# Keeping each group of column-half matmuls together in a kernel that schedules itself

## The chip, the cores and the metric

The kernel runs on one core of a Trainium2 chip. The metric is the device time of one execution in microseconds. Before the change it was 297.04 us (median of three runs, 296.97 to 297.3). A program on one core has no second die to compare with, so a run counts as slow when it is over 1.5% above the fastest of the same kernel. The granted clock is the share of its full speed that TensorE was given; 1.0 is full.

## The reference, cut to what matters

```python
# q, k, v: (4 batches, 4 heads, 1088 positions, 32); S1, S2: (8, 32)
def phi(x):                                   # 64 features of a position and head
    a = np.einsum('rd,bhsd->bhsr', S1, x)
    b = np.einsum('rd,bhsd->bhsr', S2, x)
    return np.einsum('bhsi,bhsj->bhsij', a, b).reshape(*x.shape[:-1], r * r)
q_p, k_p = (phi(q), phi(k))
kv = np.einsum('bhsf,bhsd->bhfd', k_p, v)     # "k'v"
num = np.einsum('bhsf,bhfd->bhsd', q_p, kv)   # "numerators"
den = ...                                     # denominators
x = (num / den), heads side by side           # (4, 1088, 128)

theta = x @ w_theta                           # then a mixing over the positions
zr, zi = x * np.cos(theta), x * np.sin(theta)
y = np.einsum('ts,bsd->btd', w_tok_r, zr) + np.einsum('ts,bsd->btd', w_tok_i, zi)
u = x + y
return u + np.maximum(u @ w_ch, 0.0)
```

The inputs arrive as float64 and are converted on the chip. The largest is w_tok, 1088 x 1088 twice. Its 34 pieces become the tile `wT`, in three steps of ScalarE and two of VectorE each.

## The kernel before

The kernel doesn't issue its instructions as it names them. It records them as operations, with a cost and a due time each, and a small model of the engines' time then builds the order: the engine's next operation is the one that is due first among those that could start within WAIT of the earliest.

```python
class Operation:
    def __init__(self, engine, call, args, kw, n, cost, late, due):
        self.engine, self.call, self.args, self.kw, self.n = engine, call, args, kw, n
        ...
# duration(), the model's cost of an fp32 matmul: a 64-column half has its own
            return (n / 1200 + 0.03 if ins[0].shape[1] == 64 else max(0.22, n / 600)), 0.3
...
# lay_out(): the choice, and the issue at its end
                    t, op = min(((t, o) for t, o in starts if t <= first + self.WAIT),
                                key=lambda x: (x[1].due, x[1].n))
...
        for op in out:
            r = [x.real() if isinstance(x, View) else x for x in op.args]
            op.call(*r, **{k: x.real() if isinstance(x, View) else x for k, x in op.kw.items()})
```

Two kinds of matmuls use half of TensorE's columns: k'v and numerators. In both, the two halves n = 0 and n = 1 can run side by side (in the trace of the kernel before, those of a whole pair start 6 to 8 ns apart, and a whole numerator pair takes 0.79 us to the next start, where a half alone takes 0.80). A k'v group is six such matmuls (three chunks of 128 positions, two halves), and there are 12 groups, four batches by three. A numerator pair is two, and there are 12 pairs.

```python
            for i in range(GC):                       # keys_values: GC = 3
                for n in range(2):
                    c = g * GC + i
                    T.matmul(kv[n * 2 * D:(n + 1) * 2 * D], vn[:, c, 2 * n:2 * n + 2]...,
                             kp[:, i * H + 2 * n:i * H + 2 * n + 2]...,
                             start=(c == 0), stop=(c == NC - 1), tile_position=(0, n * 2 * D), ...)
...
        for n in range(2):                            # numerator
            T.matmul(xp[n * 2 * D:(n + 1) * 2 * D], kvbd[b % 2][:, n], qpT[n],
                     start=True, stop=True, tile_position=(0, n * 2 * D), ...)
```

## Time and profile before

| | before |
|---|---|
| span of the profiled run | 295.5 us |
| TensorE busy | 257.6 us, 87% |
| VectorE busy | 224.8 us, 76% |
| ScalarE busy | 166.0 us, 56% |
| granted TensorE clock, mean | 0.912 |
| chain that ended last | 74% TensorE, 15% VectorE, 7% ScalarE |

The lines behind this table stand in the prediction. In the trace's rows, TensorE's records of fp32 matmuls come two to a matmul (a row `x12` of k'v is six matmuls), except for transpositions (`w<-ident,...`), which are one each. All operations carry one source line, since a helper records them, so one goes by the tiles' names: `w<-feat,big` is k'v, `w<-fT,kvbd` numerators, `w<-wT,st` and `w<-wT,z` the mixing, `w<-ident,feat` the transposition of features.

### The profile page before, as it was taken

How to read it: one execution, taken by the hardware profiler on the slowest of the kernel's cores; microseconds unless marked ns; L12 is line 12 of the kernel's file. 1: busy time of each engine (PE TensorE's matmuls, PEld its weight loads, DVE VectorE, ACT ScalarE, POOL GpSimd, SP SyncE). 2: the span in 40 equal slices, each digit the busy share in tenths (PEclk: the TensorE clock that was granted, in tenths of full speed). 3: DMA queues.
4: the chain of work that ended last, by engine and by line, in shares of the span. 5: the costliest groups of instructions: out<-in, count | busy, mean ns of one | idle time of the engine just before them, and what ended most of it. 6: DMA issues, size and time to landing. Idle time of an engine off the chain costs nothing.

```text
span 295.5 us, 3773 instructions
## 1 busy us (share of the span) xinstructions
PE 257.6 (87%) x1255; PEld 168.1 (57%) x1255; DVE 224.8 (76%) x638; ACT 166.0 (56%) x326; POOL 0.7 (0%) x6
## 2 busy tenths in 40 slices
PE   4539584945599999999999999999999999999993
PEld 3426553524477656656565545677656666665671
DVE  5999999999998999979999447999881994421011
ACT  3696579999528999789992223226734004620000
POOL 0000000000000000000000000000000000000000
PEclk9957867775559999999999999999999999999999
DMA  7999115967002166753300000110000001000010
GB/s 252 384 355 353 21 67 201 332 239 226 0 0 83 31 205 220 223 151 106 131 1 27 27 2 0 41 36 1 23 2 0 27 0 29 22 0 0 27 29 22
DMA packets 11603, 28.77 MB, mean 97 GB/s; under 512 B 1216, under 2 KB 5568, under 8 KB 11584
## 3 DMA queue, kind: packets, MB, share of 16 engines
q1 hardware_dynamic: 11584, 28.53, 28.7%
q8 instruction: 10, 0.16, 0.2%
q14 instruction: 9, 0.07, 0.1%
HBM read 26.30 MB, written 2.23 MB: 97 GB/s over the span
## 4 chain that ended last, share of the span: by engine, by line
PE 74%; DVE 15%; ACT 7%; DMA 1%; issue 1%; ACTq 0%
PE w L344 74%; ACT step L344 3%; DVE big L344 2%; DVE wT L344 2%; DVE lv L344 2%; DMA big<-k_l 1%; ACT big L344 1%; DVE cut_r L344 1%; DVE ksl L344 1%; DVE feat L344 1%; ACT lv L344 1%; ACT wT L344 1%; ACT tn L344 1%; DVE cut_z L344 1%; ACT fT L344 1%
## 5 line engine op out<-in xcount | busy, mean ns | idle before, releaser
L344 PE MATMUL w<-wT,st 128*128 128x384 f32 (+1 forms) x384 | 130.9, 473 | 0.0
L344 PEld LDWEIGHTS w<-wT,st 128*128 128x128 f32 x384 | 68.3, 190 | 36.9 <-issue 5.2
L344 ACT ACTIVATE step<-st 128x544 f16<-128x544 f32 (+2 forms) x70 | 54.4, 827 | 5.7 <-DVE wT L344 5.6
L344 ACT COPY ot<-w 128x384 f32<-128x384 f32 (+2 forms) x16 | 6.0, 394 | 62.6 <-PE w L344 50.4
L344 DVE TENSOR_TENSOR uT<-xT,w 128x384 f32<-128x384 f32 (+1 forms) x12 | 6.4, 530 | 28.0 <-PE w L344 27.9
L344 PE MATMUL w<-feat,big 128*64 128x128 f32 x144 | 18.3, 325 | 7.5 <-DVE feat L344 7.5
L344 DVE CUSTOM_DVE_ANT_0 wT<-wT,step 128x1088 uint16<-128x1088 uint16 x34 | 24.3, 719 | 0.7 <-ACT step L344 0.3
L344 ACT ACTIVATE wT<-st 128x544 f32<-128x544 f32 x34 | 23.6, 713 | 0.4 <-DMA st<-w_tok 0.4
L344 ACT COPY fT<-w 128x384 f32<-128x384 f32 x36 | 16.2, 490 | 9.9 <-PE w L344 9.9
L344 ACT COPY lv<-w 128x384 f32<-128x384 f32 x36 | 16.1, 500 | 8.3 <-PE w L344 8.0
L344 PEld LDWEIGHTS w<-feat,big 128*64 128x64 f32 x144 | 11.1, 156 | 15.1 <-DVE feat L344 8.2
L344 PE MATMUL w<-ident,big 128*128 128x128 f32 x72 | 13.8, 346 | 6.7 <-ACT big L344 4.2
L344 PE MATMUL w<-s_bd,fT 128*128 128x64 f32 x72 | 13.7, 353 | 6.1 <-DVE s_bd L344 6.1
L344 PE MATMUL w<-mv,qsl 128*128 128x384 f16 (+2 forms) x108 | 16.2, 290 | 1.6 <-ACT lv L344 1.3
L344 PEld LDWEIGHTS w<-s_bd,fT 128*128 128x128 f32 x72 | 12.7, 264 | 6.9 <-DVE s_bd L344 6.2
L344 PEld LDWEIGHTS w<-ident,big 128*128 128x128 f32 x72 | 11.5, 185 | 8.4 <-ACT big L344 4.6
L344 DVE TENSOR_SCALAR wT<-wT 128x544 int32<-128x544 int32 x34 | 14.5, 435 | 0.4 <-ACT wT L344 0.3
L344 PE MATMUL w<-ksl 128*128 128x384 f16 x72 | 14.6, 362 | 0.0
L344 PEld LDWEIGHTS <-qsl 128*128 128x128 f16 x108 | 9.9, 99 | 7.8 <-issue 4.5
L344 PE MATMUL w<-fT,kvbd 128*64 128x384 f32 x48 | 13.3, 542 | 0.2 <-ACT fT L344 0.2
L344 DVE SCALAR_TENSOR_TENSOR tt<-tn,w 128x384 f32<-128x384 f32 x12 | 6.6, 552 | 8.6 <-ACT tn L344 8.4
L344 PE MATMUL w<-ident,feat 128*128 128x128 f32 x72 | 12.9, 302 | 0.3 <-ACT big L344 0.3
(190 smaller groups left out, 402.1 us busy)
## 6 DMA issues: line engine op xcount, KB each, us to landing
st<-w_tok SPq DMA_DIRECT2D x34, 544.0 KB, 4.9
big<-k_l SPq DMA_DIRECT2D x4, 576.0 KB, 4.9
big<-q_l SPq DMA_DIRECT2D x4, 576.0 KB, 3.9
big<-v_l SPq DMA_DIRECT2D x4, 576.0 KB, 5.4
out<-ot SPq DMA_DIRECT2D x8, 192.0 KB, 2.1
out<-ot SPq DMA_DIRECT2D x4, 128.0 KB, 1.8
st<-w_sq SPq DMA_DIRECT2D x1, 256.0 KB, 4.9
out<-ot SPq DMA_DIRECT2D x4, 32.0 KB, 1.8
```

What stands on the lines that cost most here:

```text
L344: op.call(*r, **{k: x.real() if isinstance(x, View) else x for k, x in op.kw.items()})
```

## The change

The intent: a group's matmuls become one operation of the scheduler, so nothing can be put between the halves that run side by side. Its tuned constants were tuned again.

```diff
-START = 101.9, 134.2, 165.1, 246.3
+START = 100.5, 125.1, 182.6, 273.6
-SOONER = {"denominators0": 4.5, "denominators1": -11, ...
+SOONER = {"denominators0": 78.5, "denominators1": -44.5, ...     (all entries are new; cut)
-PACE = 2.9
+PACE = 2.4
-    WAIT = 0.08
+    WAIT = 0.02
 class Operation:
-        self.engine, self.call, self.args, self.kw, self.n = engine, call, args, kw, n
+        self.engine, self.n, self.parts = engine, n, [(call, args, kw)]
...
-            return (n / 1200 + 0.03 if ins[0].shape[1] == 64 else max(0.22, n / 600)), 0.3
+            return max(0.22, n / 600), 0.3                    (a half has no cost of its own any more)
...
+    @contextmanager
+    def together(self, cost):
+        self.joined = []
+        yield
+        op, self.joined = self.joined[0], None
+        op.cost = cost
...
     def note(self, engine, fn, call, a, kw):
+        if self.joined:
+            op = self.joined[0]
+            op.parts.append((fn, a, kw))
+        else: ...                                            (a new Operation, as before)
...
-            op.stream = min(cost, math.prod(out.shape[1:]) * passes / 2400)
+            op.stream += math.prod(out.shape[1:]) * passes / 2400 * min(1.0, out.shape[0] / 128)
...
         for op in out:
-            r = [x.real() if isinstance(x, View) else x for x in op.args]
-            op.call(*r, ...)
+            for call, args, kw in op.parts:
+                r = [x.real() if isinstance(x, View) else x for x in args]
+                call(*r, ...)
...
+            with order.together(0.81):                       # around the six k'v matmuls
...
+        with order.together(0.85):                           # around the two numerator matmuls
```

## The prediction

> **What bounds the kernel now.** I read the page first: the busy shares and the slices, which also show the granted clock.
>
> ```profile
> PE 257.6 (87%) x1255; PEld 168.1 (57%) x1255; DVE 224.8 (76%) x638; ACT 166.0 (56%) x326; POOL 0.7 (0%) x6
> PE   4539584945599999999999999999999999999993
> DVE  5999999999998999979999447999881994421011
> ACT  3696579999528999789992223226734004620000
> PEclk9957867775559999999999999999999999999999
> ```
>
> There are two regimes. For about eleven slices (7.4 us each) VectorE is full and TensorE is half idle[...]. From slice 12 on TensorE never rests. The chain of waits and a table of stretches put the border near 77 us:
>
> ```profile
> 76.61 0.59 ACT big L344
> 77.24 47.45 PE w L344 x235
> ...
> 142.53 72.52 PE w L344 x344
> 215.08 74.06 PE w L344 x300
> ```
>
> ```profile
> 62.70:90.00 27.30, 17.83 (x79) 14.49 (x79) 27.14 (x86) 17.77 (x38) 0.00 (x0) 0.50 0.25 86
> 90.00:142.00 52.00, 51.73 (x274) 33.19 (x272) 47.86 (x104) 47.80 (x91) 0.00 (x0) 1.00 0.49 154
> ```
>
> The columns after the stretch are PE, PEld, DVE, ACT, POOL and the clock. In 90 to 142 us TensorE (51.7 of 52 us), VectorE (47.9) and ScalarE (47.8) are all nearly full: VectorE and ScalarE convert the 34 pieces of w_tok into wT, and the mixing of batch 0 follows close behind. Its last rows start as the last piece is done:
>
> ```profile
> 149.54 0.44 DVE L344 TENSOR_SCALAR wT<-wT 128x544 int32<-128x544 int32 x1 [0.25 <-ACT wT L344]
> 150.72 0.72 DVE L344 CUSTOM_DVE_ANT_0 wT<-wT,step 128x1088 uint16<-128x1088 uint16 x1
> ```
>
> ```profile
> 151.02 0.81 PE L344 MATMUL w<-wT,z 128*128 128x384 f32 x2
> ```
>
> So the end is the time at which TensorE gets enough work, plus TensorE's remaining work.
>
> **What whole and broken groups cost.** From TensorE's timeline (each fp32 matmul is two records):
>
> ```profile
> 110.89 0.87 PE L344 MATMUL w<-fT,kvbd 128*64 128x384 f32 x4
> 111.68 2.74 PE L344 MATMUL w<-wT,st 128*128 128x384 f32 x8
> ...
> 128.16 0.86 PE L344 MATMUL w<-fT,kvbd 128*64 128x384 f32 x2
> 128.96 0.83 PE L344 MATMUL w<-ksl 128*128 128x256 f16 x5
> ```
>
> A numerator pair left whole takes 111.68 - 110.89 = 0.79 us; one half of a broken pair takes 0.80 us alone. In the records the halves of a whole pair start 7 ns apart. For k'v, start to next start at full clock is 0.81 us for six (at 51.59 us), 0.58 for three, 0.37 for two, 0.36 for one. A lone one also slows its neighbour:
>
> ```profile
> 162.83 0.91 PE L344 MATMUL w<-wT,st 128*128 128x384 f32 x2
> 163.67 0.43 PE L344 MATMUL w<-feat,big 128*64 128x128 f32 x2
> ```
>
> 0.84 us from start to start, where such a matmul takes 0.65 inside a run.
>
> [...] the trace grants 0.50 through 62.7 to 90 us, after TensorE had waited 4.0 us (at 68.6) and before it waits 4.2 us (at 77.2).
>
> **The change, part by part.** No instruction is added or removed: each engine keeps its counts. The new order shows all 12 k'v groups as six matmuls in a row and all 12 numerator pairs adjacent; before, only 3 groups and 10 pairs were. The scheduler's constants (SOONER, START, PACE, WAIT, the costs of these operations) change too, and with them nearly the whole order on every engine.
>
> (a) Joining, in the stretch where TensorE is full. Batch 2's k'v (91 to 100.5 us) is in eight pieces: 0.31+0.37+0.58+0.37+0.59+0.37+0.58+0.58 = 3.75 us against 3 x 0.81 = 2.43: 1.3 us. Batch 3's (162 to 181 us) is nine single ones, two twos and a five: 9 x 0.36 + 2 x 0.37 + 0.80 = 4.8 against 2.4: 2.4 us. Two broken pairs of batch 1: 4 x 0.79 = 3.2 against 1.6: 1.6 us. Sum 5.3 us; slowed neighbours add some 1.5 us. Batches 0 and 1 would save 1 us before 77 us, where TensorE waits anyway.
>
> (b) The order. I summed durations down each queue: for every kind its median start-to-start time in the trace, for TensorE at full clock. This is arithmetic that I check on the kernel before. VectorE's sum to the first query feature of batch 0 is 81.0 us, which ended at 83.9; to the last wT piece 145.4, which ended at 151.4. TensorE's sum is 229.5 us in all, and start minus sum is 54.3 us at 90.4 us, 55.4 at 126.5, 56.3 at 153, 61.1 at 289.7: nearly constant, so TensorE lost nearly all its idle time before 90 us.
>
> In the new order VectorE's sum to the first query feature is 81.4 us: the head doesn't shorten, and TensorE's dense part again begins near 84 us. By then TensorE's queue has 31.0 us of work behind it, against 33.1 before. VectorE's sum to the last wT piece falls from 145.4 to 131.0, because keys' features of batches 1 and 2, two of batch 2's preparations and batch 1's numerators come after it. With the 4 to 5 us of waits seen before that is 135.5 us. ScalarE gives the same: 41 us of its work lie between the second piece of batch 1's query slices (some 92.5 us; before 91.7) and the last conversion step, so 133.6 us without one wait, 136 with before's 2 to 3 us.
>
> TensorE's new queue puts the last rows of batch 0's mixing after a sum of only 72.1 us. It can be there by 84.3 + (72.1 - 31.0) + 3 us of low clock = 128.4 us, but the wT pieces they need come at about 134.5 us. So TensorE starves about 6 us between 98 and 135 us. Start minus sum is then 62.5 us, where before had 55.8 at the same time.
>
> After that, VectorE's and ScalarE's sums run just ahead of TensorE: batch 2's keys are sliced at 140.1 + 5 = 145 us, where TensorE arrives at 147. I add 1 to 2 us of waits there. The drift to the end was 5 us; without broken groups some 3.3.
>
> Sum: new total 223.5, its last matmul starts at sum 222.6; 222.6 + 62.5 + 3.3 + 1.5 = 289.9 us, against 289.7 before. The tail (295.5 - 289.7 = 5.8 us) has the same instructions. The span is then 295.7 us, and 297 us with the 1.5 us between span and time (297.04 - 295.5). The saving of 6 to 7 us is real, and the starving takes it back. My sums for the wT chain are good to some 2 us and lean on waits copied from before; a schedule that was tuned again was probably tuned to something better, so I put the middle at 295.5.
>
> **Rivals.** *The saving shows in full* (289 to 291 us): TensorE bounds the kernel after 77 us, so 6.5 us off its work is 6.5 us off the end. For it: the chain is TensorE from 142 to 289 us. Against: the new order asks for wT 15 us sooner than VectorE and ScalarE delivered it, with both already at 92% in that stretch. *The new order keeps low clock longer* (300 to 303 us): TensorE pauses at 68 to 84 us again and then has only small matmuls and transposes, which in 77 to 90 us ran at 0.50[...]. *Waiting for the group's last input* costs: a whole group waits for one VectorE product, and all six had the same one before; so nothing.
>
> **Range and chances.** Two us on the wT chain, two on the waits after 135 us and one on the head make about 3 us of spread: 290.5 to 300.5. Two per cent is 5.9 us: faster than 291.1 needs rival one nearly whole, 0.15; slower than 303 needs the clock to fall as well, 0.04.
>
> **What would show it.** Joined groups: 0.81 and 0.80 us each, TensorE's busy time at full clock down by 5 to 7 us. The last wT add near 136 us instead of 151.4. TensorE waits for wT between 98 and 136 us adding to about 6 us, some hidden inside matmul records; the first query feature near 84 us. The prediction is wrong if wT is done by 131 us, if TensorE has no waits there, or if the dense part begins before 80 us (then faster), or if the clock is below 1.0 after 100 us (then slower).

## The result

The changed kernel takes 293.70 us (median of four runs, 292.15 to 294.78), against 297.14 us of the kernel before in the same rounds (296.97 to 297.3). The ratio is 0.988, with a 95% interval of 0.9835 to 0.9926: under 2%, and inside the predicted range. Ratios here are the mean time of one kernel's fast runs over that of the other's of the same rounds, so they are not quite the ratio of the medians quoted.

The page of the changed kernel, busy times and slices as before:

```profile
PE 243.5 (84%) x1255; PEld 160.0 (55%) x1255; DVE 226.4 (78%) x638; ACT 164.5 (56%) x326; POOL 0.7 (0%) x6
PE   4787962631067999999999999999999999999993
DVE  5999999999999899999999875798972993611011
ACT  4797859597299899997876214008734004720000
PEclk9959998595568899999999999999999999999999
```

TensorE is busy for 14.1 us less with the same 1255 records. Part of that is the joining; that less was done at half clock (the mean clock is 0.928, before 0.912) would be the other part, which I didn't separate. In the row of slices TensorE does more early on and nothing in slice 11 (73 to 80 us), and it is full from slice 14 on, before from slice 12. ScalarE has eight or nine tenths in slices 12 to 18, where it had 2 in slice 12 and 7 and 8 in slices 17 and 18. TensorE's timeline (start, length, operation, the idle time before it and what ended it) where its dense part begins:

```profile
82.01 2.18 PE L361 MATMUL w<-ident,feat 128*128 128x128 f32 x9 [10.62 <-DVE feat L361]
...
87.19 0.94 PE L361 MATMUL w<-w,xT 128*128 128x128 f32 x6 [0.70 <-ACT xT L361]
...
90.72 0.46 PE L361 MATMUL w<-mv,qsl 128*128 128x192 f16 x3 [1.13 <-ACT qsl L361]
...
92.16 0.53 PE L361 MATMUL w<-mv,qsl 128*128 128x384 f16 x3 [0.64 <-ACT lv L361]
...
97.76 1.46 PE L361 MATMUL w<-wT,st 128*128 128x384 f32 x4
...
101.61 0.82 PE L361 MATMUL w<-feat,big 128*64 128x128 f32 x12
102.36 0.55 PE L361 MATMUL w<-ident,big 128*128 128x128 f32 x3
```

A whole k'v group is one row of twelve records with 0.75 us to the next start. The first transposition of a query feature starts at 82.01 us. In the kernel before it starts at 84.13 us, and no pause follows it up to 98 us:

```profile
84.13 1.91 PE L344 MATMUL w<-ident,feat 128*128 128x128 f32 x8
...
98.00 0.91 PE L344 MATMUL w<-mv,qsl 128*128 128x384 f16 x6
```

In the changed kernel come four waits for ScalarE (the fourth is of 0.35 us at 93.04). The clock is 0.50 in 65.5 to 86.0 and again in 92.8 to 96.2 us. From 97.76 us on TensorE has no pause until 132.52 us, and that one is of 0.24 us:

```profile
132.52 0.38 PE L361 MATMUL w<-dg,ones 8*128 8x8 f32 x2 [0.24 <-ACT fT L361]
```

The last wT addition of VectorE starts at 132.81 us (150.72 before):

```profile
132.81 0.72 DVE L361 CUSTOM_DVE_ANT_0 wT<-wT,step 128x1088 uint16<-128x1088 uint16 x1
```

The chain of waits, here its pieces around the border (start, length, what):

```profile
130.08 0.82 ACT step L361
...
132.15 0.33 ACT fT L361
...
132.52 68.10 PE w L361 x386
```

Before, TensorE carried most of the chain from 77 us on. Now ScalarE's conversions and copies carry most of it from 97 to 132.5 us (one load of w_tok stands in it with 6.0 us, before 130.08; ScalarE worked meanwhile and paused for 0.36 us), and TensorE only after that. A table of the stretch from 78 to 131 us (length, then busy time of PE, PEld, DVE, ACT, POOL, then clock, DMA share and GB/s), first before, then after:

```profile
78.00:131.00 53.00, 52.73 (x267) 35.61 (x266) 49.09 (x114) 43.07 (x85) 0.00 (x0) 0.89 0.37 118
```

```profile
78.00:131.00 53.00, 46.11 (x205) 29.43 (x206) 50.77 (x95) 51.52 (x90) 0.00 (x0) 0.89 0.58 198
```

ScalarE is busy 51.52 of 53 us. In this stretch the new order does more of w_tok's conversion and less of TensorE's work: VectorE ends 23 of the 34 pieces between 78 and 131 us, before 13, and between 78 and 98 us 8, before 4.

To see where time is won or lost, I use the prediction's measure: the start of a TensorE operation minus the sum of all full-clock TensorE work queued before it. It grows only when TensorE waits, is slow, or loses time to its neighbours. The work of each kind of matmul is its median time to the next start at full clock.

| at | before | after | difference |
|---|---|---|---|
| first transposition of a query feature (84.1; 82.0 us) | 51.1 | 51.1 | 0 |
| about 98 us | 54.5 | 58.7 | +4.2 |
| about 133 us | 55.7 | 59.2 | +3.5 |
| last matmul (289.7; 285.8 us) | 61.1 | 63.3 | +2.2 |

The sum itself fell from 228.6 to 222.6 us at the last matmul. So 6.0 us of work went and 2.2 us of other loss came: 3.8 us, and the spans differ by 295.5 - 291.6 = 3.9 us. The new order loses its 4 us between 82 and 98 us, and gets some 2 us of them back later.

### The profile page after: what moved, and what is told of

Same layout as the page of the kernel before. It is cut to its first block, busy times and chain, and to the rows that moved or that the text cites.

```text
span 291.6 us, 3787 instructions
## 1 busy us (share of the span) xinstructions
PE 243.5 (84%) x1255; PEld 160.0 (55%) x1255; DVE 226.4 (78%) x638; ACT 164.5 (56%) x326; POOL 0.7 (0%) x6
## 4 chain that ended last, share of the span: by engine, by line
PE 55%; DVE 24%; ACT 13%; DMA 4%; issue 3%; SPq 0%; ACTq 0%; DVEq 0%
PE w L361 55%; ACT step L361 6%; DVE big L361 3%; DVE wT L361 3%; ACT wT L361 2%; DMA st<-w_tok 2%; DVE feat L361 2%; DVE lv L361 2%; DMA big<-k_l 2%; ACT tn L361 2%; DVE cut_r L361 2%; DVE m L361 1%; DVE cut_z L361 1%; ACT qsl L361 1%; DVE ksl L361 1%
## 5 line engine op out<-in xcount | busy, mean ns | idle before, releaser
L361 PE MATMUL w<-wT,st 128*128 128x384 f32 (+1 forms) x384 | 127.5, 473 | 0.0
L361 PE MATMUL w<-mv,qsl 128*128 128x192 f16 (+2 forms) x108 | 18.7, 324 | 13.2 <-DVE mv L361 11.0
L361 PEld LDWEIGHTS <-qsl 128*128 128x128 f16 x108 | 11.3, 108 | 19.9 <-issue 14.5
L361 PEld LDWEIGHTS w<-ident,feat 128*128 128x128 f32 x72 | 8.9, 152 | 15.4 <-DVE feat L361 11.3
L361 DVE TENSOR_REDUCE m<-big 128x4 f32<-128x1152 f32 x8 | 10.7, 1347 | 2.3 <-DMA big<-k_l 2.3
L361 PE MATMUL w<-s_bd,fT 128*128 128x64 f32 x72 | 11.7, 300 | 0.8 <-ACT ks L361 0.6
L361 PE MATMUL w<-w,xT 128*128 128x128 f32 x72 | 11.3, 294 | 0.8 <-ACT xT L361 0.7
L361 PEld LDWEIGHTS w<-w,xT 128*128 128x128 f32 x72 | 10.0, 203 | 3.5 <-ACT xT L361 1.8
L361 PEld LDWEIGHTS w<-ident,big 128*128 128x128 f32 x72 | 9.3, 159 | 4.8 <-DMA big<-k_l 2.8
L361 PEld LDWEIGHTS w<-s_bd,fT 128*128 128x128 f32 x72 | 10.5, 214 | 2.4 <-ACT ks L361 1.1
```

## The experiments

Theory A says that joining pays directly where TensorE is full, and that the new order costs some of it. Rival B says that the new constants bring the gain and the lone halves were hidden. Theories D to H are about the loss between 82 and 98 us. Each call of runs timed the kernel before on the same chip (its median was 296.6 to 297.4 us), so I compare ratios. For the changed kernel the ratio is 0.988. The kernel before takes from 296.3 to 298.9 us, mostly near 296.6 or 298.5 us; so medians can move by half a microsecond, and one profiled run is not the median.

### 1. The old order, groups joined in place

```diff
+        last = {op.group: i for i, op in enumerate(out) if op.group}
+        joined = {}
+        for op in out:
+            joined.setdefault(op.group, []).append(op)
+        out = [x for i, op in enumerate(out) if not op.group or i == last[op.group]
+               for x in (joined[op.group] if op.group else [op])]
         for op in out:                       # the issue, as before
```

Each k'v group and each numerator pair carries a label. Its early members move back to its last one. Assertions in the code hold that no operation passed over depends on a moved one or reuses its buffers.

> The kernel before with its order on every engine kept, but each k'v six and each numerator pair put together where its last member stood. Theory A (joining pays directly where TensorE is full): from the first query feature on, TensorE's summed full-clock work falls from 196.6 to 191.2 us, and four fewer wide matmuls follow a lone half (some 0.19 us each), so 5.4 to 6.2 us off the time: 290.9 to 291.7 us, 2 us faster than the changed kernel, whose new order would then have cost that much. Rival B (the lone halves lay in time in which TensorE would have waited anyway; the gain of the change is from its new constants): 296 to 298 us. Rival C (an early member that moves back to its group's last one delays what waits for the group, or the released slots): slower than 298 us.

Measured: 292.17 us (290.87 to 292.8, six runs), ratio 0.982 (0.978 to 0.985; the limit of 2% lies inside, so the verdict is unclear between "faster" and "same"). Of the expected 5.4 to 6.2 us, 5.2 came. Batch 3's k'v, whose pieces before were nearly all single:

```profile
166.69 0.88 PE L355 MATMUL w<-feat,big 128*64 128x128 f32 x12
167.49 1.56 PE L355 MATMUL w<-wT,st 128*128 128x384 f32 x4
...
169.74 0.88 PE L355 MATMUL w<-feat,big 128*64 128x128 f32 x12
```

Theory A stands, with no constant changed; B and C fall. This kernel's median is also 1.5 us below the changed kernel's. Its interval and the changed kernel's (0.978 to 0.985, and 0.983 to 0.993) overlap a little, so I call it at least as good, and not shown to be faster.

### 2 and 3. Only k'v, only the numerators

The same edit, with the label on one kind only.

> The kernel before with only the k'v sixes put together in place. TensorE's work from the first query feature falls from 196.6 to 192.8 us (3.8 us), and four fewer wide matmuls follow a lone half (0.8 us). Theory A: 3.8 to 4.6 us off 297.4, so 292.8 to 293.6 us, most of what both parts gave (5.2 us). Rival: if only the numerator pairs' joining counts, 297 us.

Measured: 293.69 us, ratio 0.988 (0.985 to 0.991), against 297.0 us: 3.3 us off, a little under the 3.8 to 4.6 expected.

> The kernel before with only the two broken numerator pairs put together in place. TensorE's work falls by 2 x 0.80 = 1.6 us, no slowed neighbours change. Theory A: 295.8 us (1.6 us off 297.4), and the two parts together make up the 5.2 us of both. Rival: the pairs are broken where TensorE waits for wT anyway (one lone half stands at 128 us): 297 us.

Measured: 295.79 us, ratio 0.995 (0.992 to 0.998): 1.2 us off, expected 1.6. The parts add up to 4.5 us, both together gave 5.2. By the ratios, which use means, it is 3.7 and 1.6 us, together 5.3, against 5.4 for both: the parts add up. Each part pays by itself, and k'v pays most.

### 4. Joined, with the old constants

```diff
-START, SOONER, PACE, WAIT of the changed kernel
+START, SOONER, PACE, WAIT of the kernel before
```

> The changed kernel's code with the old SOONER, START, PACE and WAIT: groups are joined, but the scheduler builds an order that was never tuned. TensorE's work from the first query feature is 192.2 us (before 196.6, changed 192.6). Theory A: 291 to 295 us, the 4.4 us of work less or more some 2 us for an order that isn't tuned. Rival B (the new constants bring the gain): 296 us or more.

Measured: 316.88 us (315.3 to 318.26), ratio 1.065. Neither expectation holds: the groups are whole, TensorE's summed work is the same 223.5 us as in the changed kernel, and the time is 20 us longer than before. TensorE's timeline shows where the first of it goes:

```profile
82.63 0.90 PE L360 MATMUL w<-ident,big 128*128 128x128 f32 x3 [8.75 <-ACT big L360]
88.37 2.51 PE L360 MATMUL w<-ident,feat 128*128 128x128 f32 x9 [3.13 <-DVE cz L360]
```

The first query feature is transposed at 88.4 us, and start minus sum grows from 66.5 at 136 us to 80.0 at 192 us, where the kernel before grew by 3 (TensorE pauses for 7.3 us there and has two stretches of 3.4 us at half clock). I had taken "an order that isn't tuned" for a matter of 2 us. It is one of 20. So a scheduler that works with whole groups needs other constants than the old ones, though the new ones don't bring the gain.

### 5. Split, with the new constants

```diff
 kernel before
-START, SOONER, PACE, WAIT of the kernel before
+START, SOONER, PACE, WAIT of the changed kernel
```

> The kernel before (every half an operation of its own, with its old costs) with the new SOONER, START, PACE and WAIT. The scheduler then breaks seven of 12 k'v groups and five pairs. TensorE's work from the first query feature is 198.1 us against the changed kernel's 192.6, and 13 wide matmuls follow a half instead of 5. Theory A: 5.5 + 1.5 us more than the changed kernel, 299 to 302 us. Rival B (the gain is the constants'): 293 to 295.5 us.

Measured: 306.46 us (306.27 to 307.03), ratio 1.030. B falls again. A's direction holds and its size is short by 4 us or more. Start minus sum is 61.0 at 105 us and 69.5 at 280 us, against 58.7 and 62.5 in the changed kernel, so here too the order suffers beyond the broken groups. Constants tuned for one granularity don't carry to the other, either way.

### 6. The new order, groups broken at issue

```diff
-        for op in out:
-            for call, args, kw in op.parts:
+        (a joined operation's first part is issued at its place; part j is issued after the
+         j-th later TensorE operation, or at once when an operation comes that depends on it
+         or takes over one of its buffers)
```

> The changed kernel with its order kept, but each group broken where it is issued: between two halves comes the next other matmul of TensorE, wherever nothing depends on the half and no buffer that it reads is reused in between. 43 of 72 k'v halves then stand alone and all 24 numerator halves. TensorE's work from the first query feature rises from 192.6 to 207.5 us, and nine more wide matmuls follow a half (0.19 us each). Theory A: 15 to 17 us more than the changed kernel, 308 to 311 us. Rival B (halves are hidden): 293 to 297 us. If it is well under 308, TensorE's dense stretch holds idle time that the records hide.

Measured: two fast runs, 317.35 and 317.27 us (ratio 1.066), two slow ones, and the profile is of a slow one (323.1 us). More than A expected. The profile shows that A was right for what follows the first query feature and wrong before it. The timeline, first the new wait's end, then broken groups:

```profile
94.88 2.18 PE L379 MATMUL w<-ident,feat 128*128 128x128 f32 x9 [10.61 <-DVE feat L379]
...
115.94 0.43 PE L379 MATMUL w<-feat,big 128*64 128x128 f32 x2
116.30 0.91 PE L379 MATMUL w<-wT,st 128*128 128x384 f32 x2
117.15 0.43 PE L379 MATMUL w<-feat,big 128*64 128x128 f32 x2
```

A lone k'v matmul takes 0.36 us to the next start, and the wide one after it 0.85 us. From the first transposition to the end of the span it is 321.2 - 94.9 = 226.3 us, against 291.6 - 82.0 = 209.6 us: 16.7 us more, and the expectation's 14.9 + 9 x 0.19 was 16.6. The other 12.9 us come before: VectorE's waits from 20 to 70 us add to 12.3 us, 6.6 of them in two waits for one product of TensorE (in the changed kernel they add to 0.2 us). I had counted broken groups in the head as free, since TensorE has idle time there. That was wrong, because VectorE, which has next to none, waits for their result. As the trace is of a slow run and the fast ones are some 6 us shorter, neither share is exact. The clock is 1.0 from 98.9 us on, so the slow run's lower clock (mean 0.904, in the fast ones 0.934 and 0.935) lies before that; an estimate for the head of the fast runs is 317.3 - 293.7 - 16.7 = 6.9 us.

### 7 and 8. Filler matmuls against the low clock, in the changed order

```diff
                 op = T.transpose(tr[:, i * P:(i + 1) * P], ...)      # first query feature
+                if (b, g, n, i) == (0, 0, 0, 0):
+                    op.parts[:0] = [(nc.tensor.matmul, (tr[:, :P], ident, ident),
+                                     dict(start=True, stop=True))] * 22      # then: * 38
```

> The changed kernel with 22 matmuls of the identity by itself put before the first transposition of a query feature (their result is overwritten), in the 10.6 us in which TensorE waits there (71.4 to 82.0 us). Theory D (the changed kernel's own loss between 82 and 97 us is low clock, granted 0.50 through 82 to 86 and 92.8 to 96.2 us[...]): the clock is 1.0 from about 79 us on, and 1 to 3 us come off: 291 to 292.7 us. Rival E (VectorE and ScalarE, not the clock, set when TensorE gets its work there): the clock rises and the time stays at 293.7 us. If the filler's end comes after 82 us or its slot frees late: slower.

> The changed kernel with 38 instead of 22 identity matmuls. The 22 took 6.85 us and left 4.0 us of idle time before the first query feature, and the clock fell back to 0.50 for 81.8 to 85.2 us. Sixteen more at 0.22 us fill 3.5 us of that. Theory D: the clock stays at 1.0 through 82 to 96 us and another 1 us comes off the 293.2 us of the shorter filler, 292 us or less. Rival E: the clock stays up and the time is within 0.5 us of 293.2 us, because VectorE and ScalarE set the pace there. If the filler ends after 82 us: slower by what it is late.

Measured: 293.17 us, ratio 0.986 (0.983 to 0.989), and 293.15 us, ratio 0.987 (0.984 to 0.990). Neither is distinguishable from 0.988, though the intervals don't exclude a gain of a microsecond. The long one's timeline:

```profile
71.22 10.50 PE L361 MATMUL w<-ident 128*128 128x128 f32 x76
82.03 1.48 PE L361 MATMUL w<-ident,feat 128*128 128x128 f32 x9 [0.32 <-DVE feat L361]
84.13 1.22 PE L361 MATMUL w<-fT,kvbd 128*64 128x384 f32 x4 [0.62 <-ACT fT L361]
...
87.22 0.94 PE L361 MATMUL w<-w,xT 128*128 128x128 f32 x6 [1.39 <-ACT xT L361]
```

The clock was 1.0 through 75.1 to 92.2 us (without filler it is 0.50 in 65.5 to 86.0 us, and TensorE's records fill 4.68 of the 20.30 us from 65.6 on) and the nine transpositions took 1.48 instead of 2.18 us. Then TensorE waited for ScalarE that much longer: the xT product starts at 87.22 us, with low clock at 87.19. Rival E holds: the clock was not what kept TensorE back there. (The short filler had 1.0 also in 92.8 to 96.2 us, and its trace is 1.2 us ahead at the first wT matmuls, 96.52 against 97.76. Its six runs don't confirm a gain of that size.)

### 9 and 10. Filler matmuls in the joined old order

```diff
+            for _ in range({210: 9, 232: 12}.get(count, 0) if op.engine == "PE" else 0):
+                self.nc.tensor.matmul(r[0], ident, ident, start=True, stop=True)
             # second form: {210: 9, 232: 10}, into tile[:, 384:] of the tile written last
```

> The kernel before with both kinds of groups joined in place, and with filler matmuls of the identity in its waits: nine before the key transpositions for which TensorE waits 4.2 us until 76.6 us, twelve before the first transposition of a query feature. There the clock was 0.50 from 62.1 to 89.4 us. Theory D: the clock is 1.0 from about 76 us on, TensorE's work from 83.5 to 89.4 us (6 us at half speed) shrinks by up to 3 us: 289.2 to 291 us. Rival E (VectorE, full from 66 to 91 us, sets the pace there): 292.2 us as without the filler. If the clock doesn't rise and the filler stands in the way (2.6 to 5 us of matmuls before 83.5 us): 293 us or more.

> As the joined kernel with filler before, with the filler where it waits for no buffer: nine identity matmuls into the unused columns of the tile that TensorE wrote last, before the key transpositions for which it waits until 76.6 us, and ten before the first query feature. Theory D: the nine run from 72.3 to 76.3 us, the clock is 1.0 from about 76 us on, the ten fit before 83.5 us, and the 6 us of work at half speed after that shrink by 1.5 to 3 us: 289.2 to 290.7 us. Rival E (VectorE sets the pace up to 91 us): 291.7 to 292.5 us, as joined without filler. If the first filler runs on past 76.6 us, it holds up VectorE as in the last trial and costs 1 us or more.

Measured: 297.73 us, ratio 1.001, and 294.22 us, ratio 0.990, against 0.982 without filler. Both cost time, by my placing. In the first the filler started only at 77.72 us, after TensorE's wait of 4.22 us for ScalarE that it was meant to fill, and VectorE then waited 3.13 us for TensorE. In the second the first nine ran at once (72.75 us), and the clock went from 0.51 in 71.8 to 75.2 us to 1.00 after it. It was 0.50 again from 82.0 us on, after 3.40 us in which short matmuls filled 2.34 us, and the ten others ran at that clock from 83.98 to 88.36 us, in the way. Theory D was not tested there as I meant to. What both runs do show is that a delay of TensorE before its dense part is paid for at the end, in part: the first transposition of a query feature came 8.1 us later (91.67 against 83.52) and the time grew by 5.6 us; in the second it came 4.8 us later (88.36), and the time grew by 2.1 us.

### 11. The first query features sooner, in the changed order

```diff
+        dve = [op for op in out if op.engine == "DVE"]
+        for n in (278, 280, 282, 284, 286, 288, 289):      # dn, dn, rd, rd, fl, feat, feat
+            op = dve[n]
+            out.remove(op)
+            out.insert(out.index(dve[277]), op)            # before six wT operations
```

> The changed kernel with seven operations of VectorE issued earlier: the steps from the denominators to the first two query features of batch 0 come before the six wT operations among them (start to next start 0.35 + 0.63 + 0.63 + 0.29 + 0.35 + 0.63 = 2.9 us), which then end 2.9 us later at the most. Theory F (VectorE's queue up to the first query feature sets when TensorE's dense part starts, and nothing after it takes that back): the first feature starts near 78.1 instead of 81.0 us and the time falls by 2 to 3 us, 290.7 to 291.7 us. Theory G (the prediction's wT chain has no slack: TensorE reaches the last rows of batch 0's mixing at 130 us, when wT is done at 133 us, so what comes sooner at 82 us is waited for there): within 1 us of 293.7 us, with new waits for wT, or for ScalarE behind it, between 100 and 135 us.

Measured: 295.58 us (295.17 to 296.78), ratio 0.996. Both expectations miss. VectorE had the features 2.1 us sooner, and TensorE lost 2 us:

```profile
79.87 2.18 PE L369 MATMUL w<-ident,feat 128*128 128x128 f32 x9 [8.46 <-DVE feat L369]
87.34 1.91 PE L369 MATMUL w<-fT,kvbd 128*64 128x384 f32 x4 [5.28 <-ACT fT L369]
```

The copies fT stand in ScalarE's queue behind conversions of w_tok, and these waited for the wT operations that I had moved back. ScalarE's timeline has both:

```profile
81.71 2.78 ACT L369 ACTIVATE step<-st 128x544 f16<-128x544 f32 x4 [11.02 <-DVE wT L369]
...
86.84 0.82 ACT L369 COPY fT<-w 128x384 f32<-128x384 f32 x2
```

TensorE had written what the first of these copies reads by 82.1 us. So ScalarE ran this copy 4.7 us after it was ready, when the conversions before it in the queue were done.

### 12. Half of the conversion, in the changed order

```diff
+        light = (from 77 us on: ScalarE's two step conversions, VectorE's shift and addition of w_tok)
+        half = lambda x, op: x.real()[:, :x.shape[1] // 2] if op in light else x.real()
```

Its output is wrong, which doesn't matter for the time.

> The changed kernel with its order kept and a wrong result on purpose: from 77 us on, ScalarE's two step conversions and VectorE's shift and add of each piece of w_tok treat half of the columns only. TensorE's work is the same. Theory H (VectorE and ScalarE, full from 78 to 133 us with 51 and 52 of 53 us busy, set when TensorE's dense part starts, so the wT work pulled forward into 77 to 97 us is where the new order loses its 4 us): the first query feature comes 1 us sooner, ScalarE's copies for TensorE two to three us sooner, the first two wT matmuls of the mixing (97.8 us) start 2 to 4 us sooner, and since TensorE is full from there on, the time falls by as much: 290 to 291.5 us. Rival E2 (the loss there is TensorE's own low clock, or a chain that doesn't run over wT): 293 to 294 us. If TensorE starts sooner but then waits again for something before 135 us, the gain is smaller than the shift at 97.8 us.

Measured: 290.01 us (289.49 to 290.68), ratio 0.977 (0.974 to 0.979).

```profile
81.13 2.18 PE L365 MATMUL w<-ident,feat 128*128 128x128 f32 x9 [9.34 <-DVE feat L365]
...
94.33 1.46 PE L365 MATMUL w<-wT,st 128*128 128x384 f32 x4
```

The first wT matmuls start 97.76 - 94.33 = 3.4 us sooner, and the time is 3.7 us shorter. The table of the stretch from 78 to 131 us has ScalarE at 42.14 and VectorE at 44.73 us. Theory H stands. TensorE's work and its order were the same, so half of the conversion held TensorE back by 3.4 us at 82 to 98 us. Part of that can come through the clock, which had no second stretch of 0.50 here: where the short filler alone took that stretch away, the first wT matmuls started 1.2 us sooner. And the same cut was not tried in the old order, so how much conversion costs there is not shown; that order ends 4 pieces between 78 and 98 us, the new one 8. (This is no version to keep.)

## Why the prediction was right

The time: 293.7 us against 295.5. By its own steps:

**Joining pays in work.** Right. The sum fell by 6.0 us, and every group is whole: 0.75 to 0.81 us for six k'v, 0.80 for a pair at 139.55 us. Experiments 1 to 3 put 5.2 us of time to it in the old order, 3.3 for k'v and 1.2 for numerators taken singly. The neighbours' 1.5 us was too much. A wide matmul of 384 columns took 0.10 us longer for each side on which a half stood (0.65 us inside a run, 0.75 and 0.84 in the kernel before), beside a whole group as beside a lone one (0.74 us at 169.00 us in experiment 1); the 0.84 us that the prediction read had halves on both sides. Summed over the wide matmuls at full clock, what they take beyond runs of their like fell from 3.4 to 2.8 us, and to 2.6 us in experiment 1.

**The head doesn't shorten.** Right only in what it brings. The first transposition came at 82.0 us, 84.1 before, "near 84" predicted: VectorE had the feature 2 us sooner, though its sum had grown by 0.4 us. Its waits up to there were 3.3 us, before 4.5, and the rest is not explained. But TensorE had 2.1 us less work behind it then, so start minus sum is 51.1 us in both kernels and nothing was won.

**wT sooner.** Nearly: the last addition starts at 132.8 and ends at 133.5 us, where the prediction put 135.5. Its sum of 131.0 us was good. What failed is the 4 to 5 us of waits taken over from before; they were 2.5.

**"So TensorE starves about 6 us between 98 and 135 us."** This step failed as it was put. TensorE is busy throughout that stretch, and start minus sum grows by 0.5 us. The prediction itself named "no waits there" as a sign against it. The loss is 4.2 us and lies before: between 82 and 98 us, in 2.8 us of waits for ScalarE and half-speed work. The reason behind the step was right, the new order asks more of VectorE and ScalarE sooner. The mistake was to add up wT as a queue of its own, with TensorE running ahead to its end. ScalarE serves both in one queue: the copies without which TensorE can't go on stand between conversions (in experiment 11 a ready copy waited 4.7 us for them). So TensorE was held at the beginning and reached late pieces of wT just as they came: it has no pause there but the 0.24 us for a copy of ScalarE, and in experiment 7's trace a matmul of the mixing starts at 129.77 us, 0.05 us after the wT addition that released it. In four runs of this order (experiment 11's has the seven operations moved) its first wT matmuls started at 96.5, 97.5, 97.8 and 99.8 us, and the last wT addition 34.9 to 35.1 us later each time. Experiment 11 shows the queue, and 12 that the conversion is what holds TensorE, with the limits said there.

**The drift to the end.** 3.3 + 1.5 us predicted from there, 63.3 - 59.2 = 4.1 us measured.

**The sum.** The arithmetic gave 297 us, and "a schedule that was tuned again was probably tuned to something better" put the middle at 295.5. The error of 297 - 293.7 = 3.3 us is start minus sum at 133 us, 62.5 predicted and 59.2 measured. It is the term of wT and starving that was too large, by the waits and by the start of TensorE's part. Two smaller errors cancel: the drift was 0.7 us less than predicted, and the profiled run's time is 2.1 us above its span, not 1.5. That the middle came nearer than the sum is luck: the guess about tuning rests on no step.

**The clock.** The prediction sets the stretch of 0.50 beside TensorE's waits that ended at 68.6 and 77.2 us. The clock had fallen before both, at 62.8 us, after a stretch (59.3 to 62.8 us) in which TensorE's records fill 1.79 of 3.50 us. As a whole, TensorE is busy for 44.80 us of the first 77.24 us, at a mean clock of 0.75, and for 12.96 of the 12.96 us after that at 0.51; from 90.2 to 289 us it is busy for 198.35 of 198.80 us, at 1.00.

Of the rivals, the one of the saving in full did not come true for this kernel, but nearly did for the old order (experiment 1). That the saving was not kept in full is thus the order's doing and not the joining's. Low clock as a cause of its own did not show (experiments 7 and 8). That waiting for a group's last input costs nothing fits experiment 1, where early members moved back to it and nearly the whole saving came.

What stays open: how much of the conversion's cost the old order bears too, whether 0.982 and 0.988 are really different, and whether an order tuned by the chip rather than by the model would keep all 6 us.

## What to carry to other kernels

Matmuls that share TensorE by halves of its columns should be one unit to whatever orders them: here the broken groups cost 5 us of 297, and moving a group's early members back to its last one was enough to get that back. A scheduler's constants are tuned to its granularity, so change both together or keep the order and edit it in place. When the queue of one engine serves two chains, don't add them up apart (in experiment 11 a copy ready at 82.1 us ran at 86.84 us, behind the other chain's conversions): ask what stands before the operation that the bound engine waits for.

## More measured on wide matmuls, the clock and ScalarE's queue

- In the kernel before, a wide fp32 matmul of 384 columns takes 0.65 us to the next start inside a run of its like, 0.75 with a half on one side (165.30 us) and 0.84 with halves on both (162.83 us): 0.10 us for each such side. Beside whole groups it is the same (0.74 us at 169.00 us in experiment 1).
- In the kernel before, TensorE's records fill 3.40 of 3.40 us from 79.9 to 83.3 us, mostly with matmuls of a 128x64 operand, and the clock of the 3.40 us that follow is still 0.50. In experiment 10 the records fill 3.40 of 3.40 us from 71.8 to 75.2 us, most of it identity matmuls, and the clock is 1.00 right after. In the same run it was 0.50 after 3.40 us with 2.34 us in the records, in experiment 7 it stayed at 1.00 after 3.40 us with 1.76. So the records' busy time alone doesn't tell it.
- A copy of ScalarE that was ready at 82.1 us ran at 86.84 us (experiment 11), and the kernel lost 1.9 us although VectorE had delivered TensorE's input 2.1 us sooner.
